# Seven half products for w_in as well, in a kernel of attention and a two-layer MLP on one Trainium2 core

## The chip, the cores and the metric

The kernel runs on one core of one Trainium2 chip. The metric is device time in microseconds, the median of several runs. The core's engines appear in the profile as PE (TensorE, matmuls), PEld (TensorE loading weights), DVE (VectorE), ACT (ScalarE), POOL (GpSimd) and SP (SyncE, which only issues DMAs here).

## What is computed

The reference is softmax attention over 8 batches of 12 heads, 448 positions and 64 columns a head, then two matrix products with a leaky ReLU between them, on the 3584 tokens of all batches:

```python
def _attn_ref(q, k, v):
    scores = (1.0 / np.sqrt(64)) * np.matmul(q, k.transpose(0, 1, 3, 2))
    scores = scores - np.max(scores, axis=-1, keepdims=True)
    attn = np.exp(scores)
    attn = attn / (np.sum(attn, axis=-1, keepdims=True) + 1e-09)
    return np.matmul(attn, v)                     # (8, 12, 448, 64)

def _moe_ref(x, w_in, w_out):                     # x: (3584, 768)
    h = x @ w_in                                  # (768, 2048)
    g = np.maximum(0.01 * h, h)
    return (g @ w_out).astype(np.float32)         # (2048, 768)
```

Inputs and output are float32; the kernel multiplies in bf16 and adds up in float32.

## The kernel before

**Units and ranges.** Attention goes by units of two heads: 6 a batch, 48 in all (`NU`). The MLP goes by eight ranges of tokens that `cuts` rounds to blocks of 128: ranges 0, 2, 4 and 6 have 384 tokens, ranges 1, 3, 5 and 7 have 512. A range needs the attention of its batch and sometimes of the one before; the left-over block of ranges 0 and 4 is kept in `h` for a later pair.

**Attention.** `load` brings q, k and v of a unit: the first 18 units (`NSW`) by Pool's queue, two units to a transfer and turned into bf16 on the way, the others one by one as float32 by SP's queue. `cast` (L140) reorders them on Pool. `transposes` (TensorE) or, from unit 14 on, `dma_transposes` (L217, a DMA transpose on SP's queue) turns q and k. `scores(u, c)` (L249) computes one of four chunks of 112 keys against 448 queries for both heads, into the two halves of a PSUM tile `sc` (`ps_s`, three of them, 2 x 512 float32 each); `expo` (L261) reads both halves and writes the exponentials. `pv(u, j)` (L265) multiplies them with v for one head j, 16 matmuls of 65 columns (the 65th adds up the exponentials) into one of two PSUM banks `g`; then VectorE takes a reciprocal (L280) and multiplies (L281). `x_transposes` (L285) turns the result into `xT`, from unit 9 on by a DMA transpose on SP's queue.

**w_in's product.** `part` (L320) sums six matmuls into one bank `g` for each of 16 groups of 128 hidden columns, over all the range's tokens; ScalarE reads the bank with the leaky ReLU (L484) into `h`.

**w_out's product.** Range 0 does it plainly, in `blocks` (L442). From range 1 on `block_pair` (L374) takes two blocks of 128 tokens together and makes the four quarters of their result by seven products of half size instead of eight (Strassen's way, in the form that needs fewer sums). The sums of weights are made once, in range 1, by `mix_weights` (L333), and those of `h` by `mix_h` (L359), four VectorE instructions for each two groups. Each product is eight matmuls of 384 columns; VectorE copies the bank out (L396) or adds it to what is there (L399), and the result is stored by SP's queue.

**Order.** It is written out by hand. The main loop deals `cluster`s (L548) of attention work, three score chunks with their exponentials and the heads due, evenly over a range's matmuls, those of w_in and those of w_out alike; the third exponential waits in `late` and is issued by `settle` (L313) after the next read. Semaphores are set by the tile framework from what each instruction reads and writes.

Of the kernel before, what the change touches and what calls it, by code (L numbers as in the profile page):

```python
# [16 lines left out]
def kernel(  # L17
# [9 lines left out]
    nc = tc.nc  # L27
# [19 lines left out]
    ld_pool = ctx.enter_context(tc.tile_pool(name="ld", bufs=4))  # L47
# [8 lines left out]
    o_pool = ctx.enter_context(tc.tile_pool(name="o", bufs=3))  # L56


    ps_s = ctx.enter_context(tc.tile_pool(name="ps_s", bufs=3, space=PSUM))
    ps_g = ctx.enter_context(tc.tile_pool(name="ps_g", bufs=1, space=PSUM))  # L60

    banks = [ps_g.tile([P, 4 * P], F32, name=f"g{i}") for i in range(2)]

# [6 lines left out]
    NV = 6  # L70
# [21 lines left out]
    h_mix = h_pool.tile([P, 3, MH, 2, P], BF16, name="hmix")  # L92
# [8 lines left out]
    NSW = 18  # L101
# [7 lines left out]
    def load_soft(u, n, which):  # L109
        b, hp = divmod(u, HP)  # L110
        for x in which:
            t = ld_pool.tile([SC, 2, NSC, D], F32, name="f" + "qkv"[x])
            nc.gpsimd.dma_start(
                out=half(t)[:, :n].rearrange("p u h so d -> p (u h) (so d)"),
                in_=(q, k, v)[x][b, 2 * hp:2 * hp + 2 * n].rearrange(
                    "h (p so) d -> p h (so d)", so=NSC),
            )
            for i in range(n):
                raw.setdefault(u + i, {})[x] = half(t, i)

    def load_one(u, x, queue):
        b, hp = divmod(u, HP)
        t = ld_pool.tile([SC, 2, NSC, D], F32, name="f" + "qkv"[x])
        queue.dma_start(
            out=t.rearrange("p h so d -> p h (so d)"),
            in_=(q, k, v)[x][b, 2 * hp:2 * hp + 2].rearrange("h (p so) d -> p h (so d)", so=NSC),
        )
        raw.setdefault(u, {})[x] = t

    def load(u):  # L130
        if u >= NU:
            return
        if u < NSW:
            if u % 2 == 0:
                load_soft(u, 2, (0, 1, 2))
            return
        for x in range(3):
            load_one(u, x, nc.sync)

    def cast(u, parts=(0, 1, 2), by=nc.gpsimd.tensor_copy):  # L140
        if u >= NU:
            return
        for x in parts:
            f = raw[u].pop(x)
            if u not in qk_sb:
                qk_sb[u] = cast_pool.tile([SC, 2, NSC, 2, D], BF16, name="qkb")
            if x < 2:
                by(qk_sb[u][:, x].rearrange("p so h d -> p h so d"), f)  # L148
            else:
                by(v_sb[u % NV][:, :, :, :D], f)  # L150

# [37 lines left out]
    def stay_warm(n):  # L189

        ps = ps_s.tile([P, 2, 512], F32, name="sc", tag="sc")
        for _ in range(n):
            nc.tensor.matmul(ps[:, 0, :P], warm[:, :P], warm[:, :P], start=True, stop=True)
# [27 lines left out]
    def idle_slot():  # L221

        t = ps_s.tile([P, 2, 512], F32, name="sc", tag="sc")
        return t[:, 0], t[:, 1]

# [23 lines left out]
    def scores(u, c):  # L249
        ps = ps_s.tile([P, 2, 512], F32, name="sc", tag="sc")  # L250
        t = qkT[u % NQ]
        sc_t[u, c] = ps
        for j in range(2):
            nc.tensor.matmul(  # L254
                ps[:, j, :S],
                t[j * D:(j + 1) * D, S + c * SC:S + c * SC + P],
                t[j * D:(j + 1) * D, :S],
                start=True, stop=True,
            )
# [73 lines left out]
    def mix_weights():  # L333

        for m in range(0, MH, 2):
            lo, hi = slice(m, m + 2), slice(MH + m, MH + m + 2)
            w11, w12 = w_out_sb[:, lo, :NW], w_out_sb[:, lo, NW:]
            w21, w22 = w_out_sb[:, hi, :NW], w_out_sb[:, hi, NW:]
            t2, t3, t4 = (w_mix[:, x, lo] for x in range(3))
            for o, x, y in ((t3, w22, w12), (w12, w12, w11), (t2, w22, w12), (t4, w21, t2)):  # L340
                nc.vector.tensor_sub(o, x, y)
                yield

# [15 lines left out]
    def mix_h(i, m):  # L359
# [6 lines left out]
        h11, h21 = t[:, lo, one], t[:, lo, two]  # L366
        h12, h22 = t[:, hi, one], t[:, hi, two]
        s2, s3, s4 = (h_mix[:, x, lo, :len(at)] for x in range(3))
        nc.vector.tensor_sub(s3, h11, h21)  # L369
        nc.vector.tensor_add(h21, h21, h22)  # L370
        nc.vector.tensor_sub(s2, h21, h11)  # L371
        nc.vector.tensor_sub(s4, h12, s2)

    def block_pair(i, c):  # L374
# [4 lines left out]
        s2, s3, s4 = (h_mix[:, x, :, c] for x in range(3))  # L379
# [5 lines left out]
        b, a = next_bank(), next_bank()  # L385

        def product(ps, x, w, first=False):
            settle()
            for m in range(MH):
                nc.tensor.matmul(  # L390
                    ps[:, :NW], x[:, m], w[:, m], start=(first and m == 0), stop=(m == MH - 1), skip_group_check=True,
                )
            return MH * NW
# [7 lines left out]
        done = product(b, h[:, lo, one], w_out_sb[:, lo, left], first=True)  # L401
        keep(o1, left, b)
        yield done, None
        done = product(a, h[:, hi, one], w_out_sb[:, hi, left], first=True)
        join(o1, left, a)
        yield done, None
        done = product(b, s2, t2)
        keep(o1, right, b)
        yield done, None
        done = product(a, h[:, lo, two], t1, first=True)  # L410
        keep(o2, right, a)
        yield done, False
        done = product(b, s3, t3)
        join(o2, right, b)
        yield done, None
        t0 = token(i, x2)
        if t0 + P == B * S:
            store(o1, token(i, x1), left)
            store(o2, t0, right)
            done = product(a, s4, w_out_sb[:, hi, right])  # L420
            join(o1, right, a)
            store(o1, token(i, x1), right)
            for w in (slice(0, NW // 2), slice(NW // 2, NW)):
                for m in range(MH):
                    nc.tensor.matmul(
                        b[:, w], h[:, MH + m, two], t4[:, m, w], start=False, stop=(m == MH - 1),
                        skip_group_check=True,
                    )
                nc.vector.tensor_copy(o2[:, w], b[:, w])
                store(o2, t0, w, (nc.scalar, nc.sync))  # L430
            return
        done = product(a, s4, w_out_sb[:, hi, right])
        join(o1, right, a)
        store(o1, token(i, x1))
        yield done, None
        done = product(b, h[:, hi, two], t4)
        keep(o2, left, b)
        store(o2, t0)
        next_bank()
        yield done, True  # L440
# [21 lines left out]
    def mlp(i):  # L462

        n = cuts[i + 1] - cuts[i]
        first, pairs = spots(i)
        hs = h[:, :, first * P:first * P + n]
        if i == 0:
            for m in opened:
                part(i, m, (KD - 1,))
            for m in range(MD):  # L470
                if m not in opened:
                    part(i, m, range(KD))
                nc.scalar.activation(hs[:, m], open_t.pop(m)[:, :n], AX.Prelu, alpha=0.01)
                settle()
                yield KD * n, True
            yield from blocks(i, [(first + c, slice(w, w + NW)) for w in (0, NW) for c in range(2)])
            return

        weights = mix_weights() if i == 1 else iter(())
        ready = []  # L480
        for m in range(MD):
            mm = m // 2 + m % 2 * MH
            part(i, mm, range(KD))
            nc.scalar.activation(hs[:, mm], open_t.pop(mm)[:, :n], AX.Prelu, alpha=0.01)  # L484
            settle()
            if ready:
                mix_h(i, ready.pop())
            if m % 4 == 3:
                ready.append(m // 2 - 1)
            next(weights, None)  # L490
            yield KD * n, True
        mix_h(i, ready.pop())
        for c in range(len(pairs)):
            yield from block_pair(i, c)

# [89 lines left out]
    a, b = idle_slot()  # L585
# [19 lines left out]
    begin = [9, 8 * 2 + 3] + [8 * (i + 1) + 5 for i in range(2, B - 1)] + [8 * B + 3]  # L605

    early = [4, 6, 8, 10, 12, 14, 16, 17, 18, 19]
    for i in range(B):
        work = list(range(begin[i], begin[i + 1])) if i + 1 < B else []
        n = cuts[i + 1] - cuts[i]  # L610
        total = MD * KD * n + (len(spots(i)[1]) * 7 / 4 if i > 0 else 2) * MD * DM
        if i == B - 2:
            total *= 0.75
        used, done, groups = 0, 0, 0

        def catch_up(free):
            nonlocal done
            while done < len(work) and (
                groups >= early[done] if i == 0 else used * len(work) >= total * (done + free / 2)
            ):  # L620
                if not free and due:
                    return
                settle()
                cluster(work[done], free)
                done += 1

        catch_up(True)
        for step, free in mlp(i):
            used += step
            groups += 1  # L630
            if free is not None:
                catch_up(free)
        while due and i + 2 == B:
            finish(*due.pop(0))
# [30 lines left out]
```

## Time and profile before

| | us |
|---|---|
| median of 3 runs | 406.53 (406.39 to 407.4) |
| the profiled execution | 407.54 |
| its span, first to last instruction | 405.8 |
| TensorE busy | 393.0 (97%) |
| TensorE loading weights (beside it) | 227.1 |
| ScalarE busy | 228.3 (56%) |
| VectorE busy | 183.6 (45%) |
| GpSimd busy | 113.4 (28%) |

Span is the time from the first to the last instruction on the core. Busy is the share in which the engine had an instruction under way; matmuls overlap, so the mean time of one is more than what it adds to a stream. A group of instructions reads: line, engine, operation, output<-inputs, shapes, count | busy in all, mean ns of one | idle time of the engine just before them, and what ended it. A line of the waits reads: engine, tile and line that waited <- engine, tile and line that it waited for: us in all, times, longest. In the timeline a line starts with its start and its length in us.

The stages in the trace: w_in's product of range 1 starts at 75.2 us, its product with w_out at 104.2; that of range 7 at 362.4 and 383.1. Range 1 to the end, 330 of the 405.8 us, is what the change rewrites.

### The profile page before, as it was taken

The numbers are of one execution on the slowest core, as the hardware profiler recorded it, in microseconds if no ns is written. First come the engines' busy times: TensorE is split into PE (matmuls) and PEld (weight loads), VectorE is DVE, ScalarE is ACT, GpSimd is POOL, SyncE is SP. The second block draws the span as 40 slices with busy tenths as digits, with TensorE's granted clock in tenths as the row PEclk, the third lists the DMA queues.
The fourth block names the chain that finished last, engine by engine and source line by source line (L and its number), as shares of the span: only waits on it lengthen the run. The fifth ranks groups of instructions, "written<-read, shape, count | busy, mean of one in ns | idle before, by whom it ended". The sixth has DMA issues, their size and how long they took to land.

```text
span 405.8 us, 9155 instructions
## 1 busy us (share of the span) xinstructions
PE 393.0 (97%) x3656; PEld 227.1 (56%) x3656; DVE 183.6 (45%) x463; ACT 228.3 (56%) x324; POOL 113.4 (28%) x177
## 2 busy tenths in 40 slices
PE   7899999999999998999999999999999999999995
PEld 3566666545565655655456565554556566554453
DVE  3762433577544445434444434434344344533342
ACT  5998884577454874257644488577642585004400
POOL 8876754483303321313112132223110000000000
PEclk9999999999999999999999999999999999999999
DMA  9999998986649887666764779787716310230022
GB/s 132 196 201 204 202 201 112 222 226 170 138 122 231 197 162 151 167 152 164 145 145 107 198 186 190 158 163 183 176 39 145 91 24 13 65 94 10 2 76 79
DMA packets 96746, 57.23 MB, mean 141 GB/s; under 512 B 53312, under 2 KB 93376, under 8 KB 96704
## 3 DMA queue, kind: packets, MB, share of 16 engines
q1 hardware_dynamic: 77008, 44.15, 47.1%
q0 software_dynamic: 19392, 12.26, 21.0%
q8 instruction: 28, 0.46, 0.5%
q10 hardware_dynamic: 304, 0.25, 0.2%
q14 instruction: 14, 0.11, 0.1%
HBM read 45.61 MB, written 11.01 MB: 140 GB/s over the span
## 4 chain that ended last, share of the span: by engine, by line
PE 88%; DVE 6%; ACT 2%; issue 2%; DMA 2%; DVEq 0%; ACTq 0%; POOLq 0%
PE g L328 34%; PE g L390 28%; PE g L273 11%; PE sc L254 9%; PE g L452 3%; ACT e L263 2%; DVE x L281 2%; PE g L237 1%; DMA fq<-in_q_dram 1%; DVE rec L280 1%; PE g L294 1%; DVE hmix L371 1%; DVE o L396 1%; DVE qkb L148 0%; PE sc L328 0%
## 5 line engine op out<-in xcount | busy, mean ns | idle before, releaser
L263 ACT ACTIVATE e<-sc 112x896 bf16<-112x896 f32 x192 | 165.0, 917 | 82.5 <-PE sc L254 82.2
L328 PE MATMUL g<-xT,w_in_sb 128*128 128x512 bf16 (+1 forms) x756 | 149.7, 353 | 1.4 <-DVE x L281 1.1
L328 PEld LDWEIGHTS <-w_in_sb 128*128 128x128 bf16 x768 | 73.0, 98 | 66.1 <-issue 2.4
L484 ACT ACTIVATE h<-g 128x512 bf16<-128x512 f32 (+1 forms) x112 | 61.8, 552 | 66.6 <-PE g L328 66.6
L273 PEld LDWEIGHTS <-e 112*128 112x128 bf16 x1536 | 55.9, 98 | 22.4 <-issue 15.5
L273 PE MATMUL g<-v,e 112*128 112x65 bf16 x1536 | 63.8, 194 | 0.5 <-ACT e L263 0.2
L390 PE MATMUL g<-w_out_sb,h 128*128 128x384 bf16 x312 | 54.9, 326 | 0.9 <-DVE x L281 0.7
L390 PEld LDWEIGHTS <-h 128*128 128x128 bf16 x408 | 39.7, 98 | 27.3 <-issue 1.3
L280 DVE RECIPROCAL rec<-g 112x4 f32<-112x4 f32 x96 | 17.4, 181 | 78.7 <-PE g L273 34.4
L254 PE MATMUL sc<-qkT 64*128 64x448 bf16 x384 | 49.8, 353 | 1.1 <-DVE qkT L243 0.6
L148 POOL CAST qkb<-fq 112x512 bf16<-112x512 f32 x30 | 19.2, 639 | 99.7 <-DMA fq<-in_q_dram 80.0
L396 DVE COPY o<-g 128x384 f32<-128x384 f32 x51 | 28.4, 557 | 34.4 <-PE g L390 34.4
L390 PEld LDWEIGHTS <-hmix 128*128 128x128 bf16 x312 | 29.8, 98 | 24.5 <-issue 5.8
L281 DVE TENSOR_TENSOR x<-g,rec 112x256 bf16<-112x256 f32 x96 | 40.8, 424 | 3.3
L390 PE MATMUL g<-w_mix,hmix 128*128 128x384 bf16 x208 | 38.1, 326 | 1.3 <-DVE o L396 1.3
L150 POOL CAST v<-fv 112x512 bf16<-112x512 f32 x30 | 20.1, 672 | 62.5 <-PE g L273 56.2
L399 DVE TENSOR_TENSOR o<-o,g 128x384 f32<-128x384 f32 x39 | 21.6, 554 | 32.3 <-PE g L390 32.0
L254 PEld LDWEIGHTS <-qkT 64*128 64x128 bf16 x384 | 14.4, 94 | 19.6 <-issue 10.2
L369 DVE TENSOR_TENSOR hmix<-h 128x512 bf16<-128x512 bf16 (+1 forms) x28 | 12.6, 450 | 21.8 <-ACT h L484 21.8
L148 POOL CAST qkb<-fk 112x512 bf16<-112x512 f32 x30 | 20.9, 695 | 3.4 <-DMA fk<-in_k_dram 2.3
L370 DVE TENSOR_TENSOR h<-h 128x512 bf16<-128x512 bf16 (+1 forms) x28 | 12.9, 460 | 15.8 <-ACT h L484 15.4
L390 PE MATMUL g<-w_out_sb,hmix 128*128 128x384 bf16 x104 | 19.0, 326 | 0.0
(51 smaller groups left out, 190.1 us busy)
## 6 DMA issues: line engine op xcount, KB each, us to landing
fk<-in_k_dram SPq DMA_DIRECT2D x31, 224.0 KB, 3.5
fq<-in_q_dram SPq DMA_DIRECT2D x30, 224.0 KB, 3.4
fv<-in_v_dram SPq DMA_DIRECT2D x30, 224.0 KB, 3.9
w_in_sb<-in_moe_w_in_dram POOLq DMA_DIRECT2D x4, 768.0 KB, 11.6
w_out_sb<-in_moe_w_out_dram POOLq DMA_DIRECT2D x4, 768.0 KB, 13.4
out_dram<-o SPq DMA_DIRECT2D x7, 336.0 KB, 3.2
out_dram<-o SPq DMA_DIRECT2D x8, 288.0 KB, 3.3
fq<-in_q_dram POOLq DMA_DIRECT2D x8, 224.0 KB, 8.2
```

The costliest lines, as they stand in the source:

```text
L148: by(qk_sb[u][:, x].rearrange("p so h d -> p h so d"), f)
L150: by(v_sb[u % NV][:, :, :, :D], f)
L254: nc.tensor.matmul(ps[:, j, :S], t[j * D:(j + 1) * D, S + c * SC:S + c * SC + P], t[j * D:(j + 1) * D, :S], start=True, stop=True,)
L263: nc.scalar.activation(e[:, :, c, :], sc_t.pop((u, c))[:SC, :, :S], AX.Exp, scale=scale)
L273: nc.tensor.matmul(ps[:, qc, :], e[:, at:at + P], vt[:, j, c, :], start=(c == 0), stop=(c == NSC - 1),)
L280: nc.vector.reciprocal(rec, ps[:SC, :, D:])
L281: nc.vector.tensor_mul(x_t[u][:, :, j, :], ps[:SC, :, :D], rec.to_broadcast([SC, NSC, D]))
L328: nc.tensor.matmul(open_t[m][:, :n], w_in_sb[:, kk, ts(m, P)], xT[:, kk, at:at + n], start=(fresh and kk == kks[0]), stop=(kk == KD - 1),)
L390: nc.tensor.matmul(ps[:, :NW], x[:, m], w[:, m], start=(first and m == 0), stop=(m == MH - 1), skip_group_check=True,)
L396: nc.vector.tensor_copy(o[:, at], ps[:, :NW])
L399: nc.vector.tensor_add(o[:, at], o[:, at], ps[:, :NW])
L484: nc.scalar.activation(hs[:, mm], open_t.pop(mm)[:, :n], AX.Prelu, alpha=0.01)
```

## The change

The seven products of half size now serve w_in too, from range 1 on. `mix_w_in` makes the sums of w_in's weights during range 0, where `mix_weights` now begins too. `mix_x` makes a range's four sums of `xT`, in place where it can, eight VectorE instructions, before the range begins. `hidden` replaces the `part` loop: for each of four groups of two times two blocks of hidden columns, seven products of six matmuls with half the range's tokens (256 or 192) each. Two groups go side by side, as two chains: one in the two banks `g`, the other in the two halves of one score tile. Between products ScalarE copies a bank out, VectorE adds the next one to it, and ScalarE applies the leaky ReLU.

Of the sums of `h`, `mix_h` makes two, and `block_pair` the other two, in place, one after each of its first two products.

The order changes. `cluster` serves range 0 alone. From then on `burst` issues three score chunks and their exponentials, only between w_out's products, as many a range as `plan` says (45 in all); `rows` does `pv` for both heads of a unit, in the two halves of a score tile, and the transpose; `advance` issues loads, casts and DMA transposes a step at a time.

All later loads go by Pool's queue as bf16, two units to a transfer. The buffers: `ld` 2 for 4, `o` 5 for 3, v 5 for 6; the first loads land in the room of the weights' sums.

The new functions and the core of the diff (the helpers of loading, and unchanged lines, are left out):

```diff
+    slots = [ps_s.tile([P, 2, 512], F32, name=f"sc{i}") for i in range(3)]
+    def next_slot():
+        slots.append(slots.pop(0))
+        return slots[-1]
...
     def scores(u, c):
-        ps = ps_s.tile([P, 2, 512], F32, name="sc", tag="sc")
+        ps = next_slot()
...
+    def mix_w_in():
+        near, far = slice(0, KH), slice(KH, KD)
+        pieces = [(ts(c, 2 * P), slice(FH + 2 * c * P, FH + 2 * (c + 1) * P)) for c in range(FH // (2 * P))]
+        for lo, hi in pieces:
+            s2, s3, s4 = (w_in_mix[:, x, :, lo] for x in range(3))
+            for o, x, y in (
+                (s3, w_in_sb[:, near, lo], w_in_sb[:, near, hi]),
+                (s2, w_in_sb[:, far, hi], s3),
+                (s4, w_in_sb[:, far, lo], s2),
+            ):
+                nc.vector.tensor_sub(o, x, y)
+                yield
+        for lo, hi in pieces:
+            nc.vector.tensor_add(w_in_sb[:, near, hi], w_in_sb[:, near, hi], w_in_sb[:, far, hi])
+            yield
+    def mix_x(i, ks):
...
+        nc.vector.tensor_sub(t3, xT[:, far, two], xT[:, near, two])
+        nc.vector.tensor_sub(xT[:, near, two], xT[:, near, two], xT[:, near, one])
+        nc.vector.tensor_sub(t2, xT[:, far, two], xT[:, near, two])
+        nc.vector.tensor_sub(t4, xT[:, far, one], t2)
...
-        h11, h21 = t[:, lo, one], t[:, lo, two]
-        h12, h22 = t[:, hi, one], t[:, hi, two]
-        s2, s3, s4 = (h_mix[:, x, lo, :len(at)] for x in range(3))
-        nc.vector.tensor_sub(s3, h11, h21)
-        nc.vector.tensor_add(h21, h21, h22)
-        nc.vector.tensor_sub(s2, h21, h11)
-        nc.vector.tensor_sub(s4, h12, s2)
+        nc.vector.tensor_sub(h_mix[:, lo, :len(at)], t[:, lo, one], t[:, lo, two])
+        nc.vector.tensor_add(t[:, lo, two], t[:, lo, two], t[:, hi, two])
+    def hidden(i):
...
+        slot = next_slot()
+        slots.pop()
+        chains = [banks, [slot[:, 0], slot[:, 1]]]
...
+        def group(chain, m):
+            b, a = (x[:, :2 * nh] for x in chain)
...
+            def product(ps, w, x, first=False):
+                for j in range(2):
+                    for kk in range(KH):
+                        nc.tensor.matmul(
+                            ps[:, j * nh:(j + 1) * nh], w[:, kk, ts(j, P)], x[:, kk],
+                            start=(first and j == 0 and kk == 0), stop=(kk == KH - 1), skip_group_check=True,
+                        )
...
+            product(b, w_in_sb[:, near, cl], xT[:, near, one], first=True)
+            c11 = fresh()
+            nc.scalar.copy(c11, b)
+            yield
+            product(a, w_in_sb[:, far, cl], xT[:, far, one], first=True)
+            nc.vector.tensor_add(c11, c11, a)
+            yield
+            product(b, s2, t2)
+            act(m, left, c11)
+            c12 = fresh()
+            nc.scalar.copy(c12, b)
+            yield
+            product(a, w_in_sb[:, near, ch], xT[:, near, two], first=True)
+            c22 = fresh()
+            nc.scalar.copy(c22, a)
+            yield
+            product(b, s3, t3)
+            nc.vector.tensor_add(c22, c22, b)
+            yield
+            product(a, s4, xT[:, far, two])
+            nc.vector.tensor_add(c12, c12, a)
+            act(MH + m, right, c22)
+            yield
+            product(b, w_in_sb[:, far, ch], t4)
+            act(m, right, c12)
+            act(MH + m, left, b)
+            yield
+        for r in range(2):
+            ms = [4 * r, 4 * r + 2]
+            todo = [group(chains[x], ms[x]) for x in range(2)]
+            for step in range(7):
+                for x in range(2):
+                    yield
+                    next(todo[x])
+                    if step == 2 and ready:
+                        mix_h(i, ready.pop(0))
...
     def block_pair(i, c):
...
-        done = product(b, h[:, lo, one], w_out_sb[:, lo, left], first=True)
+        yield
+        product(b, h[:, lo, one], w_out_sb[:, lo, left], first=True)
+        nc.vector.tensor_sub(h[:, lo, one], h[:, lo, two], h[:, lo, one])
         keep(o1, left, b)
-        yield done, None
-        done = product(a, h[:, hi, one], w_out_sb[:, hi, left], first=True)
+        yield
+        product(a, h[:, hi, one], w_out_sb[:, hi, left], first=True)
+        nc.vector.tensor_sub(h[:, hi, one], h[:, hi, one], h[:, lo, one])
         join(o1, left, a)
...
+    def rows():
+        nonlocal rows_done
+        slot = next_slot()
+        for j in range(2):
+            pv(rows_done, j, slot[:, j])
+        x_transposes(rows_done)
+        rows_done += 1
+    def burst():
+        nonlocal chunk
+        todo = [divmod(chunk + x, NSC) for x in range(3) if chunk + x < NU * NSC]
+        while rows_done <= todo[-1][0] - NE or NSC * (rows_done + 1) <= chunk - 2:
+            rows()
+        for a, c in todo:
+            scores(a, c)
+        for a, c in todo:
+            expo(a, c)
+        chunk += len(todo)
+    plan = [0, 9, 9, 9, 5, 8, 5, 0]
...
+    for i in range(1, B):
+        for step, _ in enumerate(hidden(i)):
+            if i == 1:
+                next(more, None)
+            advance()
+            if step % 4 == 2 and NSC * (rows_done + 1) <= chunk:
+                rows()
...
+        for c in range(len(pairs)):
+            for _ in block_pair(i, c):
+                advance()
+                if bursts * hooks <= at * plan[i] and bursts < plan[i]:
+                    burst()
+                    bursts += 1
...
+        if not mixed:
+            mix_x(i + 1, slice(0, 2))
+            mix_x(i + 1, slice(2, 3))
```

## The prediction

> **What bounds the kernel now.** I read the page's busy times and chain first, then the groups by form, then what TensorE waits for, then two stretches of the timeline where it does wait.
>
> ```profile
> PE 393.0 (97%) x3656; PEld 227.1 (56%) x3656; DVE 183.6 (45%) x463; ACT 228.3 (56%) x324; POOL 113.4 (28%) x177
> PEclk9999999999999999999999999999999999999999
> PE 88%; DVE 6%; ACT 2%; issue 2%; DMA 2%; DVEq 0%; ACTq 0%; POOLq 0%
> ```
>
> TensorE is busy 97% of the span at full clock and carries 88% of the chain. No other engine passes 56%. So a matmul taken out is worth its full time, but only while TensorE goes on waiting for nobody.
>
> ```profile
> L328 PE MATMUL g<-xT,w_in_sb 128*128 128x512 bf16 x384 | 85.8, 379 | 0.4 <-DVE x L281 0.4
> L328 PE MATMUL g<-xT,w_in_sb 128*128 128x384 bf16 x372 | 63.9, 326 | 1.0 <-DVE x L281 0.6 <-DMA out_dram<-o 0.2
> L273 PE MATMUL g<-v,e 112*128 112x65 bf16 x1536 | 63.8, 194 | 0.5 <-ACT e L263 0.2 <-DVE x L281 0.2
> L484 ACT ACTIVATE h<-g 128x512 bf16<-128x512 f32 x64 | 38.2, 597 | 53.6 <-PE g L328 53.6
> L484 ACT ACTIVATE h<-g 128x384 bf16<-128x384 f32 x48 | 23.6, 491 | 13.0 <-PE g L328 13.0
> ```
>
> A mean holds the pipeline's tail; the pitch from one matmul to the next is what it costs in a stream. The whole waits of TensorE on other engines after 75 us come to some 4 us; the longest lines over the span are:
>
> ```profile
> PE g L390 <- DVE o L396: 1.3, 2, 1.1
> PE g L187 <- DVE gate L181: 1.2, 1, 1.2
> PE g L328 <- DVE x L281: 1.1, 5, 0.2
> ```
>
> The timeline (start, length, engine, line) shows what a wait for the reader of a PSUM bank costs when there is one, at the end of the kernel, and, in the second fence, how VectorE follows sixteen matmuls of 65 columns:
>
> ```profile
> 398.66 1.46 PE L390 MATMUL g<-w_out_sb,hmix 128*128 128x384 bf16 x8
> 399.96 0.82 PE L425 MATMUL g<-w_mix,h 128*128 128x192 bf16 x8
> 400.16 0.56 DVE L399 TENSOR_TENSOR o<-o,g 128x384 f32<-128x384 f32 x1 [0.74 <-PE g L390]
> 400.82 0.36 DVE L429 COPY o<-g 128x192 f32<-128x192 f32 x1
> 401.24 0.82 PE L425 MATMUL g<-w_mix,h 128*128 128x192 bf16 x8 [0.45 <-DVE o L429]
> ```
>
> ```profile
> 118.00 0.69 PE L273 MATMUL g<-v,e 112*128 112x65 bf16 x16
> 118.52 1.30 PE L390 MATMUL g<-w_out_sb,h 128*128 128x384 bf16 x7
> 118.72 0.18 DVE L280 RECIPROCAL rec<-g 112x4 f32<-112x4 f32 x1 [1.36 <-PE g L273]
> 118.94 0.42 DVE L281 TENSOR_TENSOR x<-g,rec 112x256 bf16<-112x256 f32 x1
> ```
>
> From these: eight matmuls of 384 start 399.96 - 398.66 = 1.30 us apart, 0.162 each; eight of 192 take (0.82 - 0.246)/7 = 0.082 each, 0.246 being one such matmul's time. VectorE starts 0.20 after a stream ends (399.96 to 400.16), and TensorE goes on 0.06 after VectorE ends (401.18 to 401.24). The multiply ends 1.36 us after the first of sixteen 65-column matmuls starts (118.00 to 119.36), although TensorE itself is free after 0.52. Matmuls of 512 run at 0.216 (twelve in 2.75 us, less a tail of 0.379); of a stream that starts at 362.19 the sixth ends at 363.49, and ScalarE's read of it starts at 363.74, 0.25 later.
>
> **A. Matmuls saved: -15.6.** Ranges 1, 3, 5, 7 have 96 matmuls of 512 each, ranges 2, 4, 6 have 96 of 384: 384 x 0.216 + 288 x 0.162 = 129.6. After: 168 a range, of 256 or 192 columns. No row has 256; it lies between 0.082 and 0.162, and half of the 512 pitch, 0.108, is on that line. 672 x 0.108 + 504 x 0.082 = 113.9. TensorE's other work stays.
>
> **What the new order adds.** The built program's list of TensorE instructions names the semaphore that each waits for. In it the score tiles `sc0` to `sc2`, each of two halves of 512, are followed as one object: a matmul into one half waits for the last reader of the other. Before, nothing came between the two halves of a tile. Now `rows` puts the two heads of a pair in the halves, and `hidden` runs its second chain of products in the halves of another.
>
> **B. `rows`: +37.4.** The first matmul of head 1 carries a wait for VectorE's multiply of head 0. So head 1 starts 1.36 + 0.06 = 1.42 us after head 0 instead of 0.52: 0.90 idle. 35 rows remain after the opening: 31.5. TensorE is in order, so scores and products queue behind. In 7 of them VectorE first has the new in-place sum of h (128x1024; rows of 512 and 768 give 0.48 and 0.64, so 0.80 estimated) ahead of its copy or add of 0.56. The reciprocal then starts 0.20 + 0.80 + 0.56 = 1.56 after the product instead of 0.72: 7 x 0.84 = 5.9.
>
> **C. Scores after a row: +11.7.** 26 of the rows stand directly ahead of three score chunks, and the third chunk takes the row's tile. It waits until 1.42 + 1.42 = 2.84 after the row's start; TensorE reaches it at 1.42 + 0.52 + 2 x 0.223 = 2.39 (six score matmuls take 0.67). 26 x 0.45.
>
> **D. The second chain in `hidden`: +27.** Each of its seven products waits for the reader of the one before, and only the first chain's product lies between. At 512: ScalarE 0.25 + 0.60 + 0.06, less the other product's 6 x 0.108 = 0.65, leaves 0.26; VectorE's f32 add is 0.69 (0.36 at 192 and 0.56 at 384 give 0.001 a column), leaving 0.30. Four waits are for ScalarE and three for VectorE: 1.94 a pass, eight passes, 15.5. At 384, against 0.49: 0.31 and 0.33, 2.23 a pass, six passes, 13.4. Seven rows that stand in `hidden` stand in for one wait each, -2. Bounds: nil, if readers were faster than a product, and double, if ScalarE's queue of 28 reads a range slips.
>
> **E. VectorE's queue at the turns: +21.** `mix_x` adds eight sums a range (four of 0.45, four of 0.34, some 3.2 us), and weights add 32 sums by range 1, 16 of them new, of about 0.65. At the start of range 1 the queue holds 0.56 + 0.65 + 7 x 0.64 + 3.2 = 8.9 us when the last block ends, starts 0.2 later, and the row two products on needs it after 2 x 0.65 + 0.72 = 2.0: +7.1. Before ranges 5 and 6 `mix_x` comes after the last product, and its first sum waits for the last row's DMA transpose (3.1 us to landing, issued after the multiply): the next row finds VectorE 3.4 and 3.3 late. In the other ranges it delays a read of a bank by 2.2, 0.7 and 1.3. In range 0 two sums at a time stand ahead of the transposes' copies, where VectorE was busy only 15 of 43 us: 3 in all. Bounds 10 and 25.
>
> **F. Turn into w_out: +5.** The first burst's last chunk waits for the last leaky ReLU of the tile given back, about 0.5 in six ranges. In the last range no scores cover the sums of h: some 2.
>
> **G. Old gaps: -6.** From 75.2 us on, pitch times count gives 314 of 327 us; 0 to 13 of the rest, range 1's stall for the weights' mixing among it, may go. I take half.
>
> **Costed at nothing.** The exponentials move into the w_out stages: nine bursts of three at 0.917 are 25 us in a stage of over 40. Copies on ScalarE: 84 more, yet 28 reads of 0.60 fit in `hidden`'s 20 us; if not, D doubles. Of VectorE's sums of h, 56 go and 26 of 0.80 come; the third product waits for one, covered by the second's 1.30, and by nothing more if VectorE is late. 91 loads leave SP; 45 more double loads at 0.7 us go to Pool, ahead of its casts, and land in 8.2 to 9.2 us instead of 3.5. They are issued two units ahead, at some 9 us a unit; with that cover gone a burst waits for its transposes. SP's transposes and stores only get earlier.
>
> [...] Without B, C and D the sum would be about 410; the list of the built program has the waits, so I keep them. [...]
>
> **Sum.** -15.6 + 37.4 + 11.7 + 27 + 21 + 5 - 6 = +80.5 on a span of 405.8: 486.3. The median run, 406.53, lies 0.7 above that span (its profiled execution took 407.54): 487.
>
> **Rivals.** (1) Faster: TensorE stays the bound. For it: it hardly waits now, and the other engines have half their time free. Against: the listed waits. The mechanism is that readers end before TensorE asks; it decides if all waits of B to F stay under 15.6 of their 102 us. With none, 405.8 - 15.6 + 0.7 = 391. Chance 0.03. (2) Only attention's waits bite; D and E are absorbed because a late TensorE gives the readers time: 405.8 - 15.6 + 37.4 + 11.7 + 5 - 6 + 0.7 = 439. Chance 0.10. (3) VectorE's order bites in every row, not seven: 28 more x 0.84 = +23.5, 511. For it: joins, sums and `mix_x` share one queue. Chance 0.12. My forecast: 0.75.
>
> The range goes from rival 2 to a little past rival 3, 438 to 513. A measurement here tells about 0.3%, 1.2 us, from no change. Only rival 1 ends at or below that: faster 0.03, same 0.01, slower 0.96.
>
> **What would show it.** TensorE's busy share near 80%; "PE sc" waiting for the multiply 60 times and more, 0.4 to 0.9 us each; the second chain's products waiting for ScalarE and VectorE by turns; matmul sums down by 15 to 16 us; a gap near 7 us early in range 1. I am wrong if TensorE stays above 93% busy, or if its waits name the DMA or ScalarE's exponentials first.

## The result, and the profile after

| | before | after |
|---|---|---|
| median, us | 406.46 (406.19 to 407.4) | 489.12 (485.51 to 489.5) |
| span of the profiled execution | 405.8 | 487.7 |
| TensorE's granted clock, mean | 1.000 | 0.972 |

The changed kernel is slower: its time is 1.2009 of the time before, with an interval from 1.1949 to 1.2069. The forecast was 487, from 438 to 513.

The page of the changed kernel, in the order read before: busy times, the granted clock, the chain.

```profile
PE 412.0 (84%) x4160; PEld 279.3 (57%) x4160; DVE 252.3 (52%) x588; ACT 273.4 (56%) x408; POOL 142.1 (29%) x222
PEclk9999999599989999899989999999999989999999
PE 51%; DVE 20%; DMA 10%; ACT 9%; issue 5%; POOL 3%; DVEq 0%; ACTq 0%; POOLq 0%
```

TensorE fell from 97% to 84% busy and from 88% to 51% of the chain, and VectorE rose from 6% to 20% of it. No engine took TensorE's place: PEld's 57% is TensorE's own loading of weights, and ScalarE is busy 56%. So this is not a new bound but one engine waiting in turns for others. TensorE's busy time of 412 holds more than work: matmuls overlap with their tails (a product of six matmuls of 256 columns has 0.82 in the record and 0.66 to the start of the next), and some ran at a granted clock of 0.50, 27 us in all.

The waits of TensorE (engine, tile and line that waited <- what it waited for: us in all, times, longest):

```profile
PE sc L280 <- DVE x L288: 45.2, 35, 9.1
PE sc L261 <- DVE x L288: 6.2, 25, 0.2
PE sc L435 <- DVE o L462: 2.8, 14, 0.2
PE sc L435 <- DVE o L450: 2.1, 11, 0.2
```

L280 is `pv`'s matmul and L288 its multiply on VectorE: 35 waits for 35 rows. L261 is a score chunk after a row. L435 is a product in `hidden`, on the tile `sc`. Before, the longest line in this view was 1.3 us.

One row from the timeline of range 1's w_out stage (start, length, engine, line):

```profile
120.18 0.67 PE L280 MATMUL sc<-v,e 112*128 112x65 bf16 x16
120.38 0.56 DVE L510 COPY o<-g 128x384 f32<-128x384 f32 x1 [0.74 <-PE g L505]
120.96 0.18 DVE L287 RECIPROCAL rec<-sc 112x4 f32<-112x4 f32 x1
121.18 0.42 DVE L288 TENSOR_TENSOR x<-sc,rec 112x256 bf16<-112x256 f32 x1
121.66 0.67 PE L280 MATMUL sc<-v,e 112*128 112x65 bf16 x16 [0.80 <-DVE x L288]
...
123.06 0.36 PE L261 MATMUL sc<-qkT 64*128 64x448 bf16 x2 [0.25 <-DVE x L288]
```

Head 1 starts 121.66 - 120.18 = 1.48 us after head 0, although TensorE needs 0.52 for head 0. It starts 0.06 after the multiply of head 0 ends (121.60): that multiply reads one half of the tile, and head 1 writes the other. The third score chunk waits in the same way for the multiply of head 1.

The first row of range 1 is the longest wait:

```profile
79.99 0.67 PE L280 MATMUL sc<-v,e 112*128 112x65 bf16 x16
82.04 1.34 DVE L350 TENSOR_TENSOR w_mix<-w_out_sb,w_mix 128x768 bf16<-128x768 bf16 x1
83.78 0.41 DVE L380 TENSOR_TENSOR x_mix<-xT 128x512 bf16<-128x512 bf16 x1
...
89.25 0.42 DVE L288 TENSOR_TENSOR x<-sc,rec 112x256 bf16<-112x256 f32 x1
89.72 1.04 PE L280 MATMUL sc<-v,e 112*128 112x65 bf16 x16 [9.06 <-DVE x L288]
...
90.57 1.47 PE L435 MATMUL g<-xT,w_in_sb 128*128 128x256 bf16 x6
...
91.84 0.42 PE L435 MATMUL sc<-xT,w_in_sb 128*128 128x256 bf16 x1
```

Sums of w_out's weights (L350) and of x (L380 on) fill VectorE's queue, and the row's multiply, which needs 0.42, comes after them, nine us late. TensorE starts no other matmul in these 9.06 us: the products queue behind the row. The last two lines show TensorE at half clock, which the profile gives from 85.3 to 95.5 (0.50): six matmuls of 256 columns take 1.27 (90.57 to 91.84), where the next fence has 0.66.

The second chain in `hidden`, in range 7, where nothing else runs:

```profile
445.15 0.82 PE L435 MATMUL sc<-xT,w_in_sb 128*128 128x256 bf16 x6
...
445.81 0.82 PE L435 MATMUL g<-x_mix,w_in_mix 128*128 128x256 bf16 x6
...
446.06 0.69 DVE L450 TENSOR_TENSOR o<-o,sc 128x512 f32<-128x512 f32 x1
...
446.80 0.82 PE L435 MATMUL sc<-x_mix,w_in_mix 128*128 128x256 bf16 x6 [0.18 <-DVE o L450]
```

A product on `g` follows its forerunner by 0.66 (445.15 to 445.81). The next one on `sc` comes 0.99 later, after VectorE has read the other half of its tile: 0.33 is lost, of which the view counts 0.18, since a matmul's record holds its tail (0.82 for a product whose pitch is 0.66).

### The profile page after: what moved, and what is told of

It reads as the page before. It is cut to its first block, busy times and chain, and to the rows that moved or that the text cites. A ratio compares the mean times of both kernels' runs of the same rounds, so it can differ in the third digit from the quotient of the medians.

```text
span 487.7 us, 10266 instructions
## 1 busy us (share of the span) xinstructions
PE 412.0 (84%) x4160; PEld 279.3 (57%) x4160; DVE 252.3 (52%) x588; ACT 273.4 (56%) x408; POOL 142.1 (29%) x222
## 4 chain that ended last, share of the span: by engine, by line
PE 51%; DVE 20%; DMA 10%; ACT 9%; issue 5%; POOL 3%; DVEq 0%; ACTq 0%; POOLq 0%
PE g L505 25%; PE sc L435 11%; DMA fv<-in_v_dram 6%; DVE x L288 6%; PE sc L280 5%; PE g L435 5%; ACT h L424 5%; PE sc L261 4%; DVE rec L287 2%; DMA w_mix<-in_v_dram 2%; ACT o L455 2%; DVE o L462 2%; ACT o L459 2%; DMA w_in_mix<-in_k_dram 1%; DVE o L513 1%
## 5 line engine op out<-in xcount | busy, mean ns | idle before, releaser
L280 PEld LDWEIGHTS <-e 112*128 112x128 bf16 x1536 | 58.2, 98 | 57.4 <-issue 52.8
L280 PE MATMUL sc<-v,e 112*128 112x65 bf16 x1120 | 47.7, 195 | 45.2 <-DVE x L288 45.2
L424 ACT ACTIVATE h<-o 128x512 bf16<-128x512 f32 (+1 forms) x84 | 48.4, 583 | 48.8 <-DVE o L450 35.1
L435 PEld LDWEIGHTS <-w_in_sb 128*128 128x128 bf16 x672 | 63.0, 100 | 19.0 <-issue 13.0
L160 POOL COPY qkb<-fq 112x512 bf16<-112x512 bf16 x38 | 25.5, 670 | 148.3 <-DMA qkT<-qkb 115.2
L261 PE MATMUL sc<-qkT 64*128 64x448 bf16 x384 | 55.8, 357 | 7.7 <-DVE x L288 6.2
L435 PEld LDWEIGHTS <-w_in_mix 128*128 128x128 bf16 x504 | 47.8, 100 | 16.8 <-issue 12.7
L162 POOL COPY v<-fv 112x512 bf16<-112x512 bf16 x38 | 24.9, 655 | 62.5 <-PE sc L280 59.2
L505 PE MATMUL g<-w_mix,h 128*128 128x384 bf16 (+1 forms) x216 | 40.8, 335 | 0.4 <-DVE o L544 0.4
L261 PEld LDWEIGHTS <-qkT 64*128 64x128 bf16 x384 | 17.0, 94 | 32.8 <-issue 23.6
L435 PE MATMUL sc<-xT,w_in_sb 128*128 128x256 bf16 (+1 forms) x252 | 33.0, 269 | 2.7 <-ACT o L447 0.4
L435 PE MATMUL g<-xT,w_in_sb 128*128 128x256 bf16 (+1 forms) x252 | 33.3, 271 | 1.4 <-DVE o L513 1.4
L160 POOL COPY qkb<-fk 112x512 bf16<-112x512 bf16 x38 | 25.3, 667 | 22.4 <-DMA fk<-in_k_dram 22.2
L288 DVE TENSOR_TENSOR x<-sc,rec 112x256 bf16<-112x256 f32 x70 | 29.7, 425 | 2.4
L435 PE MATMUL sc<-x_mix,w_in_mix 128*128 128x256 bf16 (+1 forms) x168 | 22.0, 269 | 3.4 <-DVE o L450 2.1
```

Source lines behind the costliest of these rows:

```text
L261: nc.tensor.matmul(ps[:, j, :S], t[j * D:(j + 1) * D, S + c * SC:S + c * SC + P], t[j * D:(j + 1) * D, :S], start=True, stop=True,)
L280: nc.tensor.matmul(ps[:, qc, :], e[:, at:at + P], vt[:, j, c, :], start=(c == 0), stop=(c == NSC - 1),)
L288: nc.vector.tensor_mul(x_t[u][:, :, j, :], ps[:SC, :, :D], rec.to_broadcast([SC, NSC, D]))
L424: nc.scalar.activation(hs[:, m:m + 2, cols], x.rearrange("p (m t) -> p m t", m=2), AX.Prelu, alpha=0.01)
L435: nc.tensor.matmul(ps[:, j * nh:(j + 1) * nh], w[:, kk, ts(j, P)], x[:, kk], start=(first and j == 0 and kk == 0), stop=(kk == KH - 1), sk ...
L505: nc.tensor.matmul(ps[:, cols], x[:, m], w[:, m], start=(first and m == 0), stop=(m == MH - 1), skip_group_check=True,)
```

## The experiments

The theory is the forecast's: the losses are B, C and D, waits that come from two halves being followed as one tile, and E, the order of VectorE's queue. The rivals: the waits only fill time that something else would take anyway, or w_in's seven products cost it by themselves. In the diffs, what stands as before (`-`) is the changed kernel.

### Two tiles for a row: B

```diff
-        slot = next_slot()
         for j in range(2):
-            pv(rows_done, j, slot[:, j])
+            pv(rows_done, j, next_slot()[:, j])
```

> rows puts its two heads into the first half of one score tile and the second half of another, so that head 1 no longer waits for the multiply of head 0; all else as in the changed kernel. Theory (the waits of TensorE for the reader of the other half of one tile are what was lost): 35 rows get 0.95 us each back, some 33 us, and a clock drop or two with it: 453 us, between 445 and 462. Rival (the reader's time has to be waited for anyway, the wait only moves to the score chunks that take the tiles next): 475 to 485. Rival (the loss is the seven products themselves or VectorE's load): 489.

Measured: 452.56 (450.29 to 455.36), 36.6 under the changed kernel, where B was priced at 37.4. The clock has a share in it: the half-clock stretches add up to 14 us in this trace, for 27 in the changed kernel's (mean granted clock 0.985 for 0.972). The line "PE sc L280 <- DVE x L288" is gone from its waits, and the view begins with these:

```profile
PE sc L435 <- DVE o L450: 9.6, 14, 4.1
PE sc L261 <- DVE x L288: 9.1, 34, 1.0
```

So the wait is removed by another buffer alone: same instructions, same engines. Part of it moves on: the third chunk waits more (9.1 for 6.2), and at range 1's start a product on `sc` stands in the row's place behind VectorE's queue (4.1).

### Two tiles for the second chain: D

```diff
-        slot = next_slot()
-        slots.pop()
-        chains = [banks, [slot[:, 0], slot[:, 1]]]
+        pair = [next_slot(), next_slot()]
+        slots.pop()
+        slots.pop()
+        chains = [banks, [pair[0][:, 0], pair[1][:, 0]]]
```

> The second chain in hidden gets the first halves of two score tiles instead of the two halves of one; all else as in the changed kernel. Theory: the waits of its products for ScalarE and VectorE (26 us in the trace between products of that chain) go: 463 us, between 458 and 470. Rival (ScalarE, with 28 reads a range, or VectorE is late in hidden, whatever the tiles): over 478.

Measured: 464.72 (462.75 to 466.19), down 24.4, where D was 27. In its timeline the products of both chains follow at one pitch (the numbers of lines move by a few with each edit; L436 is the changed kernel's L435):

```profile
103.11 0.82 PE L436 MATMUL sc<-x_mix,w_in_mix 128*128 128x256 bf16 x6
103.77 0.82 PE L436 MATMUL g<-xT,w_in_sb 128*128 128x256 bf16 x6
104.42 0.82 PE L436 MATMUL sc<-xT,w_in_sb 128*128 128x256 bf16 x6
```

0.65 to 0.66 a product, on `sc` as on `g`: here the readers do end in time once they read another tile.

### Both

The two edits together.

> Both edits together: the row's heads in two tiles and the second chain in two tiles. Theory: the gains add, 33 + 24, and most of the half-clock stretches go: 428 us, between 420 and 440. Rival (the gains overlap, because one late engine stands behind both): 445 or more.

Measured: 436.63 (433.73 to 437.75). The two single gains add to 61.0; together they give 52.5. There are three score tiles, and with two of them in the chain, a row inside `hidden` has one tile for both heads again:

```profile
PE sc L280 <- DVE x L288: 15.6, 7, 8.0
PE sc L261 <- DVE x L288: 9.7, 35, 1.1
```

Seven waits instead of 35, for the seven rows in hidden stages, one of them the long one at the start of range 1. The cures of B and D compete for the same three tiles.

### w_in's product as before, the new order kept

`hidden` computes w_in's product plainly, 16 groups of six matmuls (`part`) with a leaky ReLU each; the sums of w_in and of x are gone. Rows, bursts and loads stay as in the changed kernel.

> The seven products for w_in are undone: ranges 1 to 7 make w_in's product by six full matmuls a group in the two banks, as before, without the sums of weights and of x; the new order (scores only beside w_out, rows in one score tile), the in-place sums of h and the loads stay. Theory: matmuls +15.6, the chain's waits -26, VectorE's queue at the turns and the clock drops there -15 to -20: 460 us, between 452 and 468. Rival (the new order costs everything and the seven products save their 15.6): 505.

Measured: 459.16 (458.74 to 460.07). So in this order the seven products of w_in cost 489.12 - 459.16 = 30, and all the rest of the change, the new order of attention above all, costs the other 52.5 over the kernel before. Rows still wait ("PE sc L280 <- DVE x L288: 36.9, 35, 5.3" in its waits): most of the loss has nothing to do with w_in.

### Copies in the place of DMA transposes

All runs from here on have one edit in common. They leave out the transposes of x, q and k by DMA: two plain copies of the same bytes stand for each, and values land in wrong places. They show times only, and are compared with each other. This one and the one after it show what the edit is worth.

```diff
-        nc.sync.dma_start_transpose(out=dst.rearrange("p (c s) -> p c s", s=SC), in_=src)
+        n = dst.shape[-1]
+        nc.sync.dma_start(out=dst[:SC], in_=src[:, :n])
+        nc.sync.dma_start(out=dst[SC:], in_=src[:P - SC, :n])
```

> The run with two tiles for a row's heads and two for the second chain, with one thing more: the 73 transposes that SP's DMA makes (of x and of q and k) are left out, and two plain copies of the same bytes stand for each, from partitions to the same partitions, so that queues, dependences and the work of all engines stay and only the places of the values are wrong. It shows whether the copies move the time. Theory (no one waits for SP's transfers): within 3 of the 437 with the transposes. Rival (the transposes' landing holds rows or scores somewhere): 430 or less, or over 442.

Measured: 435.82 (434.22 to 438.75), against 436.63 with transposes. And the kernel before with the same edit:

> The kernel before, with its DMA transposes left out and two plain copies of the same bytes in place of each, as in the runs above (values land in wrong places). It is the base for those runs. Theory (no one waits for SP's transfers): 406.5, within 1.5 of the kernel before, so that 405.5 with plain w_in, two tiles for a row and rows inside products is a little below it. Rival (the transposes cost something in the kernel before): 405 or less, and nothing is gained there.

Measured: 406.16 (405.72 to 408.48), ratio to the kernel before 0.9985, from 0.9967 to 1.0003. The copies move neither kernel by more than 1 us. The changed kernel itself was not run with copies.

### Later sums: E

```diff
-            for _ in range(min(4, 2 * x)):
-                next(more)
...
-            if i == 1:
+            if i == 1 and step >= 8:
                 next(more, None)
...
-            if step % 4 == 2 and NSC * (rows_done + 1) <= chunk:
+            if step % 4 == 2 and step >= 10 and NSC * (rows_done + 1) <= chunk:
```

In the changed kernel with its tiles as they are:

> The changed kernel with copies for transposes and its score tiles as they are, but all of w_out's weight sums wait until step 8 of range 1's hidden, and rows in hidden come from step 10 on. Theory (E as the forecast sized it, some 20 of queueing of VectorE): 470, between 463 and 478. Rival (E was over-sized: with two tiles the same edit gave 4.3): 480 to 487.

Measured: 478.79 (478.22 to 480.41). This fits neither expectation well: against 489.12, 10.3 came back, where the theory wanted 19 and the rival 2 to 9. In its waits the rows' line falls from 45.2 to 34.5, its longest from 9.1 to 1.9. But the moved sums stand in range 1's hidden stage, where the second chain now waits for VectorE's f32 adds (up to 1.0), and the sums of x stay ahead of products that need them (3.1 in three waits). With two tiles for rows and chain:

> Transposes by plain copies as in the run before. All of w_out's weight sums wait until step 8 of range 1's hidden, and rows in hidden come from step 10 on. Theory (E, VectorE's queue at the turns, is most of what is left of its term): 420, between 413 and 428. Rival (what is left at 437 is not the order of VectorE's work at the turns): 434 or more.

Measured: 431.51 (429.28 to 432.47), 4.3 less than without the edit: between the two again, nearer to the rival. The order of VectorE's queue can be moved cheaply, but its work lands somewhere, and each place in these stages has a reader that TensorE needs.

### Rows inside a product: C

A row that the next burst needs is issued after four of the eight matmuls of the product ahead of that burst, not just ahead of its chunks:

```diff
             for m in range(MH):
+                if m == MH // 2:
+                    between()
                 nc.tensor.matmul(
```

> The kernel of the run before (copies for transposes, later sums), and a row that a burst of scores needs is issued in the middle of the product ahead of the burst, after four of its eight matmuls, instead of just ahead of the third score chunk. Theory (C: the third chunk waits for the row's multiply because nothing of TensorE lies between them): 402, between 396 and 412. Rival (ScalarE's exponentials or the slots hold the chunks as long): 415 or more.

Measured: 422.93 (419.83 to 425.82), 8.6 less than the run before. The theory put C's gain at 18 (420 to 402), and the time lies where the rival had it, but the chunks were freed: by stages of the trace the w_out stages fall from 200.7 to 185.8 in sum, 14.9 less, and the third chunk's wait for the multiply is gone from the top of the list. But the hidden stages rise from 147.3 to 157.6:

```profile
PE sc L282 <- DVE x L290: 8.0, 7, 2.9
PE sc L438 <- ACT o L458: 5.2, 3, 2.8
PE sc L263 <- ACT h L427: 4.1, 6, 1.2
PE g L438 <- DVE x_mix L384: 3.4, 4, 1.4
```

All four lines lie at or in hidden stages: rows on the one tile that is left; the second chain waiting for ScalarE's copy; scores waiting for the last leaky ReLU of the tiles given back; and the sums of x. For the second line the view names only the last link. ScalarE's own waits give what its copy (L458) waited for:

```profile
ACT o L458 <- DMA out_dram<-o: 6.1, 3, 3.3
```

`hidden` keeps its sums in the five `o` buffers, which w_out's results leave only when their stores have ended. In the changed kernel's waits this line is missing; there, it seems, TensorE is late enough for the stores. It is a new wait behind those taken away, and a sixth buffer was not tried.

### No rows in hidden

The `rows()` call in the loop over `hidden` is taken out of the run before; bursts and idle steps take those rows.

> The run with rows inside products (two tiles for a row's heads and for the second chain, later sums, copies), with no rows in the hidden stages at all: the bursts beside w_out's product take them. Theory (what the seven products of w_in still cost is that their second chain leaves one score tile, on which a row's second head waits, 9.7 in the seven rows there): 414, between 410 and 418. Rival (the rows wait as long where they go instead, or the chain's own waits for sums and copies decide): 420 or more.

Measured: 414.84 (413.81 to 417.83), as the theory said. Hidden stages fall to 143.4 in sum, and the w_out stages, with four more rows, rise by 4.1.

### Plain w_in with all the cures

The run with rows inside products, with w_in's product as before the change (and rows in hidden again, which has free tiles then).

> The run with rows inside products, with w_in's product as before the change (no seven products, no sums of w_in and x), copies for transposes too. It asks whether w_in's seven products pay once the waits are gone. Theory (A: 15.6 saved, some of it spent at the second chain's tiles): 413, between 405 and 422, and 6 to 14 above the run with rows inside products. Rival (the seven products cost VectorE and the slots what they save): at or below that run.

Measured: 405.47 (405.2 to 406.1), ratio 0.9958, from 0.9935 to 0.9981: 17.5 below the same kernel with seven products. This is the rival's case: the theory had put the plain version 6 to 14 above the seven products, because it would lose the saved matmuls. That 405.47 lies in the range given with the theory is luck: the kernel with seven products stood at 422.93, not at the 402 expected. The new order of attention, with its waits taken away, is as good as the old one (406.16 with the same copies), and TensorE is back at 98%:

```profile
PE 394.0 (98%) x3656; PEld 224.3 (56%) x3656; DVE 172.6 (43%) x432; ACT 231.9 (57%) x324; POOL 140.8 (35%) x222
```

With plain w_in the hidden stages of ranges 1 to 7 take 141.5 in sum, their pitches alone 140.5. With seven products and the same rows they take 157.6, though their matmuls are 15.7 shorter.

### Seven products in range 7 alone

The run with plain w_in and all cures, with the seven products in range 7 only, whose hidden stage holds no rows and no scores. The sums of w_in's weights go beside w_out's products of ranges 4 to 6.

> The run with plain w_in, two tiles for a row and rows inside products (405.5), with w_in's seven products in range 7 alone, where no rows and no scores stand in the hidden stage; two tiles for the second chain there; the 16 sums of w_in's weights go beside w_out's products of ranges 4, 5 and 6; copies for transposes as before. In the runs with seven products range 7's hidden stage took 18.3, with plain ones 20.7. Theory (the matmuls saved come out in full where nothing waits): 403.1, between 402 and 404.2. Rival (the late weight sums and x sums on VectorE cost as much in the w_out stages as is saved): 405 or more.

Measured: 405.07 (404.6 to 407.16), ratio to the kernel before 0.9966, from 0.9953 to 0.9979. Against 405.47 the runs tell no difference; the rival holds. The trace shows where the saving went. The hidden stage of range 7 takes 18.3 us for 20.7, as expected: 2.4 saved, 96 x 0.216 less 168 x 0.108 = 2.6 by the pitches. But it starts 1.8 later (361.8 for 360.0):

```profile
357.82 0.56 DVE L539 TENSOR_TENSOR o<-o,g 128x384 f32<-128x384 f32 x1 [0.86 <-PE g L531]
358.29 0.42 DVE L382 TENSOR_TENSOR x_mix<-xT 128x512 bf16<-128x512 bf16 x1
...
361.18 0.55 DVE L539 TENSOR_TENSOR o<-o,g 128x384 f32<-128x384 f32 x1
```

Eight sums of x, from 358.29 to 361.26, stand ahead of the read that empties the bank, and TensorE's first product waits 1.4 for it. This is E again in small: eight sums that no idle time of the total would forbid (VectorE is 47% busy) at the one place where someone waits.

## Why the prediction was right

In the traces, the time from range 1's first matmul to TensorE's last is 405.5 us after and 327.1 before, and range 1 starts 3.7 later: 82.1 in all. Counted by the pitch from one matmul to the next, point by point:

| step | forecast | in the trace of after |
|---|---|---|
| A, matmuls | -15.6 | -15.7 (296.5 for 312.2) |
| B with the rows of E (7.1, 3.4, 3.3) | +51.2 | +50.9, 35 rows |
| C and F, gaps between score chunks | +16.7 | +15.8 |
| D, second chain | +27 | +26.0 (15.5 at 256, 10.5 at 192) |
| rest of E (7.2), G (-6), half clock (no term) | +1.2 | +5.1 |
| sum | +80.5 | +82.1 |

The signs that were named came too: "PE sc" waits for the multiply 60 times (35 and 25 in the two lines shown), and the early wait in range 1 is 9.1 for 7.

The runs stand behind B (36.6 came back for 37.4, though with E's part of the rows and the clock in it, and some waits moved on) and D (24.4 for 27). C has no run of its own with the tiles as they were; in the run with rows inside products 14.9 came back in the w_out stages, there beside two-tile rows.

**A** (its own terms give 15.7, not 15.6) came out as half of the 512 pitch: in a stretch without waits a 256-column product of six takes 0.65 to 0.66.

**B** is right in kind and size. The usual row starts head 1 after 1.47 instead of 1.42. Of the seven rows with a sum of h ahead, five take 1.96 instead of 2.26, since the sum takes 0.69, not 0.80; the other two take 2.08 and 2.46, where it took 0.81 and 1.13. That 50.9 is so near to 51.2 is luck: errors of up to 4 us, in both directions, cancel in it (the rows at the turns are under E).

**C** per chunk is 0.40 for the 0.45 forecast.

**E** is right in kind, and its parts were mis-sized both ways. The first row of range 1 takes 9.7 for 8.5 forecast: a weight sum there takes up to 1.34 where 0.65 was put in. The rows at ranges 5 and 6 take 2.9 each for 4.8. Range 0 ends 3.7 later for 3; in "Later sums", with w_out's sums moved out of it, 0.7 later. Its sum of 21 is not shown: the later sums gave back 10.3.

**G and the clock.** Apart from B, C, F and D, 16.3 us of gaps remain after range 1 begins, for 14.9 in all before. Some 9.5 of the 16.3 lie in the half-clock stretches, between matmuls that wait for nobody and start at about twice their pitch (1.27 a product for 0.66). That leaves 7. So G's gain of 6 may have come, but no run shows which gaps went: half of a remainder was taken as gain with no wait named that would go. The weak step is the clock, for which the sum has no term. The three half-clock stretches behind E's three long waits cost 5.1. Three others cost 4.3; they follow rows whose head 1 starts 2.0 to 2.5 after head 0. In all the trace has 27 us at half clock in six stretches, of which the first 4.4 lie in range 1's stall anyway. So the sum, 80.5 for 82.1, is in part luck: about as much fell away elsewhere as the clock took.

**The rivals.** That readers end before TensorE asks was wrong for the tiles as they are (45.2 us of waits for the multiply), and right for the second chain once it has two (the timeline above). "Only attention's waits bite", 439, fell: D is worth 24.4 by itself. That VectorE's order bites in every row fell too: the longer starts of head 1 stay with thirteen of the 35 rows, those with sums ahead. Without B, C and D the sum was put near 410: with separate tiles for B and D the kernel reached 435.8, and 414.84 with the other edits, so most of the distance is the tracking of tiles, as the forecast kept it.

**What the forecast did not say** is that A would not be collected even with the waits gone. Plain w_in with the cures is 9.4 below the best run with seven products in all ranges (414.84). The seven products take more than matmuls: tiles for the second chain, which rows and scores need; `o` buffers that stores still hold (4.7 in two waits of ScalarE in that run); and VectorE's queue at moments when TensorE waits for it. Whether more of 9.4 could be had by buffers or another order stays open.

## What to carry to other kernels

When TensorE is at 97% because nothing waits, count for each saved matmul the reads of PSUM that its replacement adds, and ask of each read which instruction of TensorE stands behind it and on which tile. Give what is read at different times its own tile, even where one tile has room for both: here that alone was worth 52.5 us, what it gave back at the clock included (a mean granted clock of 0.980 for 0.972). Sums that are free by an engine's busy share still have a place in its queue (eight of them, with VectorE 47% busy, held TensorE for 1.4 us before range 7), so put them where no reader of a bank that is due comes after them.

## What the hardware showed that was not expected

TensorE's granted clock fell to half after waits as short as 1.3 us. The view by windows (us, busy time and count of PE, PEld, DVE, ACT and POOL, granted clock, DMA share, GB/s), in the changed kernel:

```profile
85.30:95.50 10.20, 5.78 (x40) 4.25 (x40) 7.52 (x17) 1.49 (x3) 5.09 (x8) 0.50 0.83 97
133.10:136.50 3.40, 1.87 (x28) 1.06 (x25) 1.91 (x6) 1.10 (x2) 1.25 (x2) 0.99 1.24 205
136.50:139.90 3.40, 3.40 (x13) 1.58 (x11) 1.15 (x2) 1.87 (x3) 0.61 (x1) 0.50 1.18 197
```

From 133.1 to 136.5 TensorE was busy 1.87 of 3.40 us, its longest wait there was 1.3 us, and from 136.5 it ran 3.4 us at half clock although it was busy all the time. The six half-clock stretches of this trace begin at 85.3, 136.5, 197.9, 245.7, 327.6 and 392.5. The first lasts 10.24 us, each of the others 3.41, and from one beginning to the next it is 15, 18, 14, 24 and 19 times 3.41 us.

So the trace from 3.4 to 484.6 us can be cut into stretches of 3.41 us in which the granted clock is the same throughout. In the one just ahead of each of the six beginnings TensorE was idle for 3.41, 1.53, 1.62, 1.78, 2.26 and 2.12 us. All others at full clock had 1.52 of idle time or less, and full clock after them. The idle time of a stretch need not be one wait: the 1.53 ahead of 136.5 are a row's 1.3 and a score chunk's 0.25. Here, then, short waits, packed closely, cost a second time: the three stretches behind rows like this one cost 4.3 us.
